# Attention scores and value products as small TensorE tiles of 64 rows

## The chip, the cores and the metric

The kernel runs on one core of one Trainium2 chip. The metric is the device time of the program in microseconds, the median of several runs. One more run was profiled: the trace of that one execution is what all rows below come from. Engines are called PE (TensorE, matmuls), PEld (its weight loads), DVE (VectorE), ACT (ScalarE), POOL (GpSimd) and SP (SyncE, which issues most transfers).

## What is computed

A local attention is followed by two feed-forward layers, all in float32. Batch is 4, there are 8 heads of 64 dimensions and 768 positions. Positions are cut into chunks of 32; the queries of a chunk see 16 positions to the left, the chunk itself, 8 to the right, and 8 memory positions, 64 keys in all.

```
for c in range(nc):                       # 24 chunks
    q_c   = q[:, :, 32*c : 32*c+32]
    k_full = concat(mem_k, k[:, :, max(0, 32*c-16) : min(S, 32*c+40)])
    v_full = the same of mem_v, v
    scores = q_c @ k_full.T / sqrt(64)
    a = exp(scores - max(scores)); a = a / (sum(a) + 1e-9)
    out[:, :, 32*c : 32*c+32] = a @ v_full

x = out as 3072 tokens x 512
h = x @ w_in;  g = max(0.01*h, h);  x = g @ w_out          # 512 -> 2048 -> 512
y = ((x @ w_a) * (x @ w_b)) @ w_out2                        # 512 -> 1536 -> 512
```

## The kernel before

Tokens are cut into 24 units of 128 (four chunks each, all eight heads) and into six blocks of 512 tokens (`bi`, four units each). The first feed-forward layer runs block after block: for each of 16 slices `f` of the hidden width, `mm1` computes h (L413 to L415, three matmuls of 128x128 weights over 512 columns, four times) and, two slices later, `mm2` adds it into four accumulators a (L533 to L537). The attention of block `bi + 1` is laid between the slices of block `bi` by the table `beside` (`at(bi, f, ...)`); the attention of units 0 to 3 comes first, in an order written out by hand (`InOrder`, whose instructions all have the line L47, or L44 for the first). From unit 4 on a scheduler sets the order on each engine. From 603 us on the last layers run, which the change does not touch.

For one unit the steps are these. `a_scores` multiplies queries and keys into the PSUM tile s (L277); `a_max`, `a_exp`, `a_soft1` and `a_soft2` make the softmax on DVE and ACT in the tile p; the probabilities are turned, keys onto the partitions, into PT, for units 0 to 7 by PE and a copy of ACT (`a_turn_mm`, L357, and `a_turn_copy`, L368), for later units by 16 DVE transposes of 32x32 pieces (`a_turn`, L346); `a_pv` multiplies them with the values into the PSUM tile pv (L386); `a_out` splits that into a high part on ACT (L399) and a low part on DVE (L400), the inputs xh and xl of the next block.

Two heads are handled in one matmul, with zeros: the queries of two heads stand in the two halves of the 128 rows, each in its own 32 of 64 weight columns, and the rest of the 64 columns is zero (`qs`, `qz`, set once on POOL and DVE). One matmul of scores thus has 128 rows, 64 weight columns (two heads of 32 queries) and 64 moving columns (keys); even and odd chunks write the lower and upper 64 PSUM partitions. In the value products the 64 weight columns are the dimensions of a head, the 64 moving columns two sets of 32 queries of PT, half of each zero. One unit has 16 matmuls of each kind. Each fp32 matmul shows as two records in the trace.

PSUM has eight banks of 512 floats for each partition: two for h (`ps_h`), two that scores, turned probabilities and products of units 2 and later take in turn (`ps_s`), four that hold a and, at the start, other things (`ps_a`).

Of the kernel before, what the change touches and what calls it, by code (L numbers as in the profile page):

```python
# [14 lines left out]
P = 128  # L15
# [38 lines left out]
def kernel(  # L54
# [28 lines left out]
        for n, b in (("ps_h", 2), ("ps_s", 2), ("ps_a", 4))  # L83
    ]
    ps_h, ps_s, ps_a = [p.__enter__() for p in psum1]
# [46 lines left out]
    class Weights:  # L132
# [70 lines left out]
    qz = ap_.tile([P, 16, 2 * CH], F32, tag="qz", name="qz", bufs=1)  # L203
    qs = [
        ap_.tile([P, 2 * CH, 16], F32, tag=t, name="qs", bufs=1) for t in ("pz", "ps", "pwa", "pwb")
# [3 lines left out]
    PT = [  # L209
        ap_.tile([P, 4, 4, 2, CH], F32, tag=f"pt{i}", name=f"pt{i}", bufs=1) for i in range(2)  # L210
    ]
    for t in qs[0:2]:
        nc.gpsimd.memset(t[0:64, CH:2 * CH, :], 0.0)
        dve.memset(t[64:128, 0:CH, :], 0.0)
    for t in PT:
        nc.gpsimd.memset(t[0:64, :, :, 1, :], 0.0)
        nc.gpsimd.memset(t[64:128, :, :, 0, :], 0.0)
    for t in qs[2:4]:
        nc.gpsimd.memset(t[0:64, CH:2 * CH, :], 0.0)
        nc.gpsimd.memset(t[64:128, 0:CH, :], 0.0)  # L220
    nc.gpsimd.memset(qz[0:64, :, CH:2 * CH], 0.0)
    nc.gpsimd.memset(qz[64:128, :, 0:CH], 0.0)
# [5 lines left out]
    def q_load(upto):  # L228
        while loaded[0] < min(upto, NU):
            u = loaded[0]  # L230
            if u < len(qs):
                eng = act if u < 1 else sp
                sp.dma_start(out=qs[u][0:64, 0:CH, :], in_=q_l[u, 0:64])
                eng.dma_start(out=qs[u][64:128, CH:2 * CH, :], in_=q_l[u, 64:128])
# [9 lines left out]
    def q_place(u, copy):  # L244
        if u >= NU:
            return
        t = qr.pop(u).rearrange("p q o -> p o q")
        qb = qz
        copy(qb[0:64, :, 0:CH], t[0:64])
        copy(qb[64:128, :, CH:2 * CH], t[64:128])  # L250
# [17 lines left out]
    def a_scores(u):  # L268
        qb = q_of(u)
        s = ps_s.tile([P, 8, 64], F32, tag="s", name="s")  # L270
        for cp in range(2):
            k = kt.pop((u, cp))
            for hp in range(4):
                for cpar in range(2):
                    o = (2 * cp + cpar) * 4 + hp
                    r = (cpar * 4 + hp) * 64
                    pe.matmul(  # L277
                        s[64 * cpar:64 * cpar + 64, cp * 4 + hp, :],
                        qb[:, o, :],
                        k[:, r:r + 64],  # L280
                        start=True, stop=True,
                    )
        st[u] = s
# [4 lines left out]
    def a_max(u):  # L288
        s = st[u]
        m = sm.tile([P, 8], F32, tag="m", name="m", bufs=2)  # L290
        dve.reduce_max(m, s, axis=AX.X)
# [3 lines left out]
        else:  # L295
            dve.tensor_tensor(
                out=p, in0=s, in1=m.unsqueeze(2).to_broadcast([P, 8, 64]), op=ALU.subtract
# [3 lines left out]
    def a_exp(u):  # L301
        s = st.pop(u)
        p, m = pt_[u]
        if u in by_scalar:
            l = sm.tile([P, 8], F32, tag="l", name="l", bufs=2)
            for r in range(8):
                act.activation(
                    p[:, r], s[:, r], AF.Exp, bias=m[:, r:r + 1], scale=scale,
# [11 lines left out]
    def a_soft2(u):  # L320
        p = pt_[u]
        if u % UPB == 0:
            dve.memset(p[0:64, 0:4, 0:LEFT], 0.0)
        if u % UPB == UPB - 1:
            dve.memset(p[64:128, 4:8, WIN - RIGHT:WIN], 0.0)
# [11 lines left out]
    def a_turn(u):  # L337
        p = pt_.pop(u)
        pt = PT[u % 2]
        for cpar in range(2):  # L340
            for hpar in range(2):
                i0 = 64 * cpar + 32 * hpar
                for hpx in range(2):
                    for b in range(2):
                        o0 = 64 * hpx + 32 * b
                        dve.transpose(  # L346
                            out=pt[o0:o0 + 32, :, 2 * cpar + hpar, hpx, :],
                            in_=p[i0:i0 + 32, hpx::2, 32 * b:32 * b + 32],
                        )
# [3 lines left out]
    def a_turn_mm(u, pool, tag):  # L353
        p = pt_.pop(u)
        ps = pool.tile([P, 4, 4, CH], F32, tag=tag, name="pT")
# [8 lines left out]
    def a_turn_copy(u, halves=(0, 1)):  # L364
# [5 lines left out]
    def a_turn_pe(u, pool, tag):  # L370
        a_turn_mm(u, pool, tag)
# [4 lines left out]
    def a_pv(u, pool, tag):  # L376
        pt = PT[u % 2]
        o = pool.tile([P, KC, UT], F32, tag=tag, name="pv")
        for cp in range(2):
            v = vt.pop((u, cp))  # L380
            for pair in range(2):
                for cpar in range(2):
                    for hpar in range(2):
                        i = ((cpar * 2 + hpar) * 2 + pair) * 64
                        t0 = (2 * cp + cpar) * CH
                        pe.matmul(  # L386
                            o[64 * hpar:64 * hpar + 64, 2 * pair:2 * pair + 2, t0:t0 + CH],
                            v[:, i:i + 64],
                            pt[:, 2 * cp + pair, 2 * cpar + hpar].rearrange("p h q -> p (h q)"),
# [6 lines left out]
    def a_out(u, blk, off):  # L396
        o = pvt.pop(u)
        hi, lo = x1[blk]
        act.copy(hi[:, :, off:off + UT], o)  # L399
        dve.tensor_tensor(  # L400
# [805 lines left out]
```

## Time and profile before

| | us |
|---|---|
| median of three runs | 1138.04 (1137.56 to 1139.1) |
| the profiled execution, whole | 1137.88 |
| its span in the trace | 1136.1 |
| PE busy | 1119.5 |
| DVE busy | 805.3 |
| ACT busy | 476.2 |

The page gives for each engine its busy time and share. Busy time of PE is from a record's start to its modelled end, and records overlap, so the cost of a group is read from the starts of what stands before and behind it in the timeline.

### The profile page before, as it was taken

Reading aid. Unit: us, or ns where it says so; the run is one execution under the profiler, and the core shown is the slowest. Engines: PE = TensorE matmul, PEld = TensorE weight load, DVE = VectorE, ACT = ScalarE, POOL = GpSimd, SP = SyncE. Lnnn points to the kernel's source line nnn. Section 1 sums busy time; section 2 is a strip of 40 time slices with the busy share of each in tenths; the row PEclk is TensorE's granted clock in tenths of the full one; section 3 lists DMA queues with packets and bytes.
Section 4 is the critical chain, followed back from the end, with each engine's and each line's share of the span. In section 5 each row is a group of like instructions: output and inputs, shape, how many; then the busy total and the mean of one; then the engine's idle time right before and its main releaser. Section 6 shows DMA issues by size and latency. Waiting matters only on the chain.

```text
span 1136.1 us, 18009 instructions
## 1 busy us (share of the span) xinstructions
PE 1119.5 (99%) x6992; PEld 956.9 (84%) x6992; DVE 805.3 (71%) x1485; ACT 476.2 (42%) x806; POOL 6.3 (1%) x16
## 2 busy tenths in 40 slices
PE   6899999999999999999999999999999999999998
PEld 6788888888888888888888898988898989898988
DVE  7999499889979964645112838598747689756777
ACT  5887555565554544325223424143333143333231
POOL 2000000000000000000000000000000000000000
PEclk9999999999999999999999999999999999999999
DMA  9988799999999985336236766667756567747451
GB/s 319 390 277 305 272 350 319 320 341 340 315 329 334 331 304 180 111 96 235 97 145 229 252 209 180 199 189 254 268 174 200 173 211 227 222 153 231 147 188 74
DMA packets 89380, 269.68 MB, mean 237 GB/s; under 512 B 9552, under 2 KB 10960, under 8 KB 88528
## 3 DMA queue, kind: packets, MB, share of 16 engines
q1 hardware_dynamic: 89216, 268.41, 70.1%
q8 instruction: 55, 0.90, 0.3%
q14 instruction: 29, 0.24, 0.1%
q10 hardware_dynamic: 80, 0.13, 0.0%
HBM read 214.50 MB, written 54.00 MB: 236 GB/s over the span
## 4 chain that ended last, share of the span: by engine, by line
PE 92%; DVE 3%; DMA 2%; ACT 2%; SPq 1%; issue 0%; DVEq 0%; ACTq 0%
PE h L413 8%; PE a L533 7%; PE a L536 7%; PE a L537 7%; PE h L414 7%; PE h L415 7%; PE A L874 4%; PE A L873 4%; PE A L875 4%; PE C L874 3%; PE C L873 3%; PE C L875 3%; PE oc L1012 2%; PE oc L1011 2%; PE oc L1010 2%; PE pv L386 2%
## 5 line engine op out<-in xcount | busy, mean ns | idle before, releaser
L413 PE MATMUL h<-xh,w 128*128 128x512 f32 (+1 forms) x384 | 151.5, 394 | 1.4 <-DVE w L183 0.7
L533 PE MATMUL a<-gh,w 128*128 128x512 f32 (+1 forms) x392 | 150.6, 384 | 0.5 <-DVE w L183 0.3
L536 PE MATMUL a<-gl,w 128*128 128x512 f32 (+1 forms) x392 | 150.4, 384 | 0.0
L537 PE MATMUL a<-gh,w 128*128 128x512 f32 (+1 forms) x392 | 150.4, 384 | 0.0
L414 PE MATMUL h<-xl,w 128*128 128x512 f32 (+1 forms) x384 | 148.5, 387 | 0.2 <-DVE xl L47 0.2
L415 PE MATMUL h<-xh,w 128*128 128x512 f32 (+1 forms) x384 | 148.5, 387 | 0.0
L511 DVE TENSOR_TENSOR gl<-g,gh 128x512 fp32r<-128x512 f32 (+1 forms) x96 | 65.2, 679 | 94.0 <-ACT gh L508 93.6
L899 ACT CAST st<-gb 128x512 fp32r<-128x512 f32 x114 | 69.4, 621 | 108.7 <-DVE gb L894 108.4
L505 ACT ACTIVATE g<-h 128x512 f32<-128x512 f32 (+1 forms) x96 | 56.3, 586 | 113.0 <-PE h L415 112.3
L890 ACT COPY u<-A 128x512 f32<-128x512 f32 x68 | 39.9, 586 | 115.8 <-PE A L875 115.8
L533 PEld LDWEIGHTS a<-gh,w 128*128 128x128 f32 x392 | 73.6, 188 | 15.6 <-ACT x L550 0.6
L413 PEld LDWEIGHTS h<-xh,w 128*128 128x128 f32 x384 | 72.1, 188 | 17.2 <-DVE w L183 0.9
L536 PEld LDWEIGHTS a<-gl,w 128*128 128x128 f32 x392 | 73.6, 188 | 14.5
L537 PEld LDWEIGHTS a<-gh,w 128*128 128x128 f32 x392 | 73.7, 188 | 14.5
L894 DVE TENSOR_TENSOR st<-gb,st 128x512 fp32r<-128x512 f32 x111 | 75.3, 690 | 13.5 <-ACT st L899 11.3
L415 PEld LDWEIGHTS h<-xh,w 128*128 128x128 f32 x384 | 72.1, 188 | 14.7
L414 PEld LDWEIGHTS h<-xl,w 128*128 128x128 f32 x384 | 72.2, 188 | 14.2 <-DVE xl L47 0.5
L346 DVE STREAM_TRANSPOSE pt<-p 32x128 f32<-32x128 f32 x256 | 77.4, 302 | 4.3
L873 PE MATMUL A<-ch,wab 128*128 128x512 f32 x204 | 79.5, 390 | 0.0
L874 PE MATMUL A<-cl,wab 128*128 128x512 f32 x204 | 79.5, 390 | 0.0
L875 PE MATMUL A<-ch,wab 128*128 128x512 f32 x204 | 79.4, 389 | 0.0
L508 ACT CAST gh<-g 128x512 fp32r<-128x512 f32 (+1 forms) x96 | 59.0, 615 | 2.7
(180 smaller groups left out, 2311.1 us busy)
## 6 DMA issues: line engine op xcount, KB each, us to landing
wab<-wab SPq DMA_DIRECT2D x126, 512.0 KB, 4.3
w<-wod SPq DMA_DIRECT2D x80, 512.0 KB, 4.8
raw<-w SPq DMA_DIRECT2D x68, 512.0 KB, 6.8
wt<-wtd SPq DMA_DIRECT2D x63, 512.0 KB, 4.7
k<-kl SPq DMA_DIRECT2D x48, 256.0 KB, 5.3
v<-vl SPq DMA_DIRECT2D x48, 256.0 KB, 5.7
wab<-pwb SPq DMA_DIRECT2D x12, 768.0 KB, 6.3
wod<-w SPq DMA_DIRECT2D x16, 512.0 KB, 5.6
```

What stands on the lines that cost most here:

```text
L346: dve.transpose(out=pt[o0:o0 + 32, :, 2 * cpar + hpar, hpx, :], in_=p[i0:i0 + 32, hpx::2, 32 * b:32 * b + 32],)
L413: pe.matmul(ps, w[1], x[0], start=first, stop=False)
L414: pe.matmul(ps, w[0], x[1], start=False, stop=False)
L415: pe.matmul(ps, w[0], x[0], start=False, stop=last)
L533: pe.matmul(ps, slot[:, 1, c], gh[:, t], start=f == 0 and o == 0, stop=False, **kw)
L536: pe.matmul(ps, slot[:, 0, c], gl[:, t], start=False, stop=False, **kw)
L537: pe.matmul(ps, slot[:, 0, c], gh[:, t], start=False, stop=f == NF1 - 1 or (o == HALF and f == LEAD - 1), **kw)
L873: pe.matmul(ps, w[:, 1, c], hi[:, kc], start=first and kc == 0, stop=False, **kw)
L874: pe.matmul(ps, w[:, 0, c], lo[:, kc], start=False, stop=False, **kw)
L875: pe.matmul(ps, w[:, 0, c], hi[:, kc], start=False, stop=kc == HC - 1, **kw)
L894: dve.tensor_tensor(out=out, in0=x, in1=y, op=op)
L899: act.copy(w[:, 0, :], t)
```

## The change

Scores and products are cut into matmuls of one head and one chunk. A score matmul takes 64 rows (one head's dimensions), 32 weight columns (32 queries) and 64 moving columns (keys); a product takes 64 rows (keys), 64 weight columns (dimensions) and 32 moving columns (queries). There are 32 of each per unit. The position in the array follows from the operands: the row half from the partitions they are read from (`hpar`, or `hpx`), the column part from the PSUM partitions they write. The two row halves write two different PSUM banks. The zeros are gone, and with them the memsets and one of two copies into `qz` and into PT; the queries of units 1 to 3 come in one transfer.

PSUM is handed out in pairs of banks (`pair`). Units 0 to 3 use one pair of `ps_s` and two of `ps_p`; then `open_acc` gives the four banks of `ps_p` to the accumulators. From unit 4 on there is one pair. `cluster` puts the products of a unit and the scores of the next into one pair, products in the first half of each bank, scores in the second; the turned probabilities of units 3 to 7 use the same pair between clusters.

```diff
-        for n, b in (("ps_h", 2), ("ps_s", 2), ("ps_a", 4))
+        for n, b in (("ps_h", 2), ("ps_s", 1), ("ps_p", 2))
...
-    qz = ap_.tile([P, 16, 2 * CH], F32, tag="qz", name="qz", bufs=1)
+    qz = ap_.tile([P, 16, CH], F32, tag="qz", name="qz", bufs=1)
...
-    for t in qs[0:2]:
-        nc.gpsimd.memset(t[0:64, CH:2 * CH, :], 0.0)
-        dve.memset(t[64:128, 0:CH, :], 0.0)
...
-        copy(qb[0:64, :, 0:CH], t[0:64])
-        copy(qb[64:128, :, CH:2 * CH], t[64:128])
+        copy(qz, qr.pop(u).rearrange("p q o -> p o q"))
...
+    def pair(pool):
+        return pool.tile([P, 2, 512], F32, tag="s", name="sv")
+
+    def a_scores(u, bank, half=0):
+        qb = q_of(u)
+        s = bank[:, :, 256 * half:256 * half + 256].rearrange("p b (r k) -> p b r k", k=64)
+        ks = [kt.pop((u, cp)) for cp in range(2)]
+        for cs in ((0, 1), (2, 3)) if u < 1 else (range(4),):
+            for hp in range(4):
+                for c in cs:
+                    for hpar in range(2):
+                        d = slice(64 * hpar, 64 * hpar + 64)
+                        r = ((c % 2) * 4 + hp) * 64
+                        pe.matmul(
+                            s[32 * c:32 * c + 32, hpar, hp, :],
+                            qb[d, 4 * c + hp, :],
+                            ks[c // 2][d, r:r + 64],
+                            start=True, stop=True,
+                        )
...
-        for h in halves:
-            d = slice(64 * h, 64 * h + 64)
-            act.copy(pt[d, :, :, h, :], ps[d])
+        act.copy(pt, ps)
...
+        o = bank[:, :, 0:256].rearrange("p x (a t) -> p x a t", a=2)
+        vs = [vt.pop((u, cp)) for cp in range(2)]
+        for a in range(2):
+            for c in range(4):
+                for hpar in range(2):
+                    for hpx in range(2):
+                        i = (((c % 2) * 2 + hpar) * 2 + a) * 64
+                        d = slice(64 * hpx, 64 * hpx + 64)
                         pe.matmul(
+                            o[64 * hpar:64 * hpar + 64, hpx, a, c * CH:c * CH + CH],
+                            vs[c // 2][d, i:i + 64],
+                            pt[d, 2 * hpar + a, c, :],
                             start=True, stop=True,
                         )
...
+    def cluster(u, n):
+        bank = pair(ps_s)
+        if u is not None:
+            a_pv(u, bank)
+        if n is not None:
+            a_scores(n, bank, 1)
```

How this moves instructions is shown at three places on PE.

The first is the middle of block 1, where the products of one unit and the scores of the next stand between the slices of the feed-forward layer. In the names, h and a are its results, xh and xl its inputs, gh and gl the parts of g, w a weight; before, s and pv are scores and products, and after, sv is the pair of banks for both. Before:

```order
L537 MATMUL a<-gh,w 128x512
L386 MATMUL pv<-pt_126,v 64x2x32 x16
L277 MATMUL s<-k,qz 64x64 x16
L413 MATMUL h<-xh,w 128x512
L414 MATMUL h<-xl,w 128x512
```

And now:

```order
L530 MATMUL a<-gh,w 128x512
L374 MATMUL sv<-pt_126,v 64x32 x32
L267 MATMUL sv<-k,qz 32x64 x32
L400 MATMUL h<-xh,w 128x512
L401 MATMUL h<-xl,w 128x512
```

The place is the same; the matmuls have doubled in number, and the two kinds now have different shapes. There are 15 such places, and five each where only scores or only products stand.

The second is unit 4, on PE behind the four transposes (pT before, the rows `sv<-id,p` now) that turn its probabilities. Before:

```order
L357 MATMUL pT<-id,p 128x128 x4
L413 MATMUL h<-xh,w 128x512
L414 MATMUL h<-xl,w 128x512
L415 MATMUL h<-xh,w 128x512
```

And now:

```order
L347 MATMUL sv<-id,p 128x128 x4
L374 MATMUL sv<-pt_126,v 64x32
L400 MATMUL h<-xh,w 128x512
L401 MATMUL h<-xl,w 128x512
L402 MATMUL h<-xh,w 128x512
...
L374 MATMUL sv<-pt_126,v 64x32 x31
L267 MATMUL sv<-k,qz 32x64 x32
```

One of the 32 products of unit 4 has come forward by 24 matmuls, to right behind the transposes; the other 31 stand where all 16 stood.

The third is unit 3 in the start, with the waits that the rows carry. Before:

```order
L47 MATMUL pT<-id,p 128x128 [waits DVE_49,PE_49,Activation_49]
L47 MATMUL pT<-id,p 128x128 x3
L47 MATMUL a<-gh,w 128x256 [waits DVE_49]
L47 MATMUL a<-gl,w 128x256 [waits Activation_49]
```

And now:

```order
L47 MATMUL sv<-id,p 128x128 [waits DVE_49]
L47 MATMUL sv<-id,p 128x128 [waits Activation_49] x3
L47 MATMUL a<-gh,w 128x256
L47 MATMUL a<-gl,w 128x256 [waits Activation_49]
```

The order is the same. The transposes write the pair of banks that the products of unit 2 used, so their wait for DVE now covers the reading of those products (`a_out(2)`), which stands behind `a_soft2(3)` in DVE's order; the wait of the first a is gone, since it is met earlier.

## Rows read from the trace of the kernel before

**Rows 1.** The page: span, and busy us (share of the span) xinstructions
```profile
span 1136.1 us, 18009 instructions
PE 1119.5 (99%) x6992; PEld 956.9 (84%) x6992; DVE 805.3 (71%) x1485; ACT 476.2 (42%) x806; POOL 6.3 (1%) x16
```

**Rows 2.** PE's waits from 36 us on: us in total, times, longest
```profile
PE h L413 <- DVE w L183: 0.7, 1, 0.7
...
PE a L533 <- DVE w L183: 0.3, 1, 0.3
...
PE a L533 <- ACT x L550: 0.2, 1, 0.2
```

**Rows 3.** Groups by shape, 60 to 530 us: busy us, mean ns | idle before
```profile
L386 PE MATMUL pv<-pt,v 128*64 128x64 f32 x640 | 23.0, 225 | 0.0
...
L277 PE MATMUL s<-k,qz 128*64 128x64 f32 x608 | 21.2, 223 | 0.0
```

**Rows 4.** Timeline of PE around 70 us: start us, us, line, weights, moving, records
```profile
69.47 0.39 PE L536 MATMUL a<-gl,w 128*128 128x512 f32 x1
69.70 0.39 PE L537 MATMUL a<-gh,w 128*128 128x512 f32 x1
70.02 1.15 PE L386 MATMUL pv<-pt,v 128*64 128x64 f32 x32
71.00 1.10 PE L277 MATMUL s<-k,qz 128*64 128x64 f32 x32
72.03 0.50 PE L413 MATMUL h<-xh,w 128*128 128x512 f32 x1
72.37 0.39 PE L414 MATMUL h<-xl,w 128*128 128x512 f32 x1
```

**Rows 5.** Timeline of PE from 70.01 to 70.03 us alone
```profile
70.02 0.28 PE L386 MATMUL pv<-pt,v 128*64 128x64 f32 x2
```

**Rows 6.** Timeline of PE in the start: fillers of 128 columns
```profile
11.79 1.50 PE L47 MATMUL warm<-id 128*128 128x128 f32 x12
```

**Rows 7.** Weight loads by shape, 15 to 36 us: busy us, mean ns
```profile
L47 PEld LDWEIGHTS h<-xh,w 128*128 128x128 f32 x24 | 3.9, 189 | 1.0 <-ACT xh L47 0.9
...
L47 PEld LDWEIGHTS pv<-pt,v 128*64 128x64 f32 x96 | 3.1, 138 | 0.4 <-ACT pt L47 0.3
```

**Rows 8.** Timeline of PE at the transposes of unit 4
```profile
63.96 0.63 PE L357 MATMUL pT<-id,p 128*128 128x128 f32 x4
64.34 0.48 PE L413 MATMUL h<-xh,w 128*128 128x512 f32 x1
```

**Rows 9.** Timeline of ACT there
```profile
64.97 1.18 ACT L368 COPY pt<-pT 64x512 f32<-64x512 f32 x2
```

**Rows 10.** Timeline of PE at unit 3, in the start
```profile
30.78 0.63 PE L47 MATMUL pT<-id,p 128*128 128x128 f32 x4 [0.98 <-ACT g L47]
31.89 0.39 PE L47 MATMUL a<-gh,w 128*128 128x256 f32 x1 [0.49 <-DVE w L47]
...
33.52 1.15 PE L47 MATMUL pv<-pt,v 128*64 128x64 f32 x32
```

**Rows 11.** Timeline of DVE in the start
```profile
28.61 0.69 DVE L47 SCALAR_TENSOR_TENSOR z<-raw,z 128x512 int32<-128x512 int32 x1
29.50 0.17 DVE L47 TENSOR_SCALAR l<-l 128x8 f32<-128x8 f32 x1 [0.19 <-ACT p L47]
...
31.75 0.68 DVE L47 TENSOR_TENSOR xl<-pv,xh 128x512 fp32r<-128x512 f32 x1
```

**Rows 12.** Chain of work in the start, in order of time: start us, us
```profile
12.32 8.18 DMA raw<-w
...
26.99 2.48 ACT p L47 x16
```

**Rows 13.** Stretch 60 to 85 us: PE, PEld, DVE, ACT, POOL busy, PEclk, DMA, GB/s
```profile
60.00:85.00 25.00, 25.00 (x169) 20.48 (x168) 24.86 (x50) 20.03 (x34) 0.00 (x0) 1.00 0.89 292
```

**Rows 14.** Timeline of PE behind the scores of unit 4
```profile
44.95 0.39 PE L533 MATMUL a<-gh,w 128*128 128x256 f32 x1 [0.30 <-DVE w L183]
```

More of the change, by code (lines that the diff above doesn't have):

```diff
@@ L202 @@
     ident = sm.tile([P, P], F32, tag="id", name="id", bufs=1)
[L203 removed]
+    qz = ap_.tile([P, 16, CH], F32, tag="qz", name="qz", bufs=1)
     qs = [
[L205 removed]
+        ap_.tile([P, CH, 16], F32, tag=t, name="qs", bufs=1) for t in ("pz", "ps", "pwa", "pwb")
     ]
[L209 to L222 removed]
+    PT = [ap_.tile([P, 4, 4, CH], F32, tag=f"pt{i}", name=f"pt{i}", bufs=1) for i in range(2)]
     kt, vt, st, qr = {}, {}, {}, {}
@@ L231, in q_load @@
             if u < len(qs):
-                eng = act if u < 1 else sp
-                sp.dma_start(out=qs[u][0:64, 0:CH, :], in_=q_l[u, 0:64])
-                eng.dma_start(out=qs[u][64:128, CH:2 * CH, :], in_=q_l[u, 64:128])
+                if u < 1:
+                    sp.dma_start(out=qs[u][0:64], in_=q_l[u, 0:64])
+                    act.dma_start(out=qs[u][64:128], in_=q_l[u, 64:128])
+                else:
+                    sp.dma_start(out=qs[u], in_=q_l[u])
             else:
@@ L296, in a_max @@
             dve.tensor_tensor(
-                out=p, in0=s, in1=m.unsqueeze(2).to_broadcast([P, 8, 64]), op=ALU.subtract
+                out=p.rearrange("p (b r) k -> p b r k", b=2), in0=s,
+                in1=m2.unsqueeze(3).to_broadcast([P, 2, 4, 64]), op=ALU.subtract,
             )
@@ L339, in a_turn, with a_turn_mm @@
         pt = PT[u % 2]
[L340 to L349, printed above, removed]
+        for c in range(4):
+            for hpx in range(2):
+                for b in range(2):
+                    o0 = 64 * hpx + 32 * b
+                    dve.transpose(
+                        out=pt[o0:o0 + 32, :, c, :],
+                        in_=p[32 * c:32 * c + 32, hpx::2, 32 * b:32 * b + 32],
+                    )
     turned = {}
-    def a_turn_mm(u, pool, tag):
+    def a_turn_mm(u, pool):
         p = pt_.pop(u)
-        ps = pool.tile([P, 4, 4, CH], F32, tag=tag, name="pT")
+        ps = pair(pool)[:, 0].rearrange("p (r c q) -> p r c q", r=4, c=4)
         for r in range(4):
@@ L397, in a_out @@
         o = pvt.pop(u)
-        hi, lo = x1[blk]
-        act.copy(hi[:, :, off:off + UT], o)
-        dve.tensor_tensor(
-            out=lo[:, :, off:off + UT], in0=o, in1=hi[:, :, off:off + UT].bitcast(F32),
-            op=ALU.subtract,
-        )
+        hi, lo = [
+            x[:, :, off:off + UT].rearrange("p (a x) t -> p x a t", x=2) for x in x1[blk]
+        ]
+        act.copy(hi, o)
+        dve.tensor_tensor(out=lo, in0=o, in1=hi.bitcast(F32), op=ALU.subtract)
     def x_tiles(key):
@@ L442 @@
     q_load(3)
-    warm = ps_a.tile([P, TB], F32, tag="a", name="warm")
+    warm = ps_h.tile([P, TB], F32, tag="h", name="warm")
     def fill(n):
@@ L448, in fill @@
             pe.matmul(warm[:, 0:P], ident, ident, start=True, stop=True)
-    a_scores(0)
-    a_scores(1)
+    a_scores(0, pair(ps_s))
+    a_scores(1, pair(ps_p))
     fill(6)
@@ L462 @@
     a_soft2(0)
-    a_turn_mm(0, ps_a, "a")
+    a_turn_mm(0, ps_p)
     fill(6)
     a_max(1)
-    a_turn_copy(0, (0,))
+    a_turn_copy(0)
     a_exp(1)
-    a_turn_copy(0, (1,))
     W1.bias(2)
-    a_pv(0, ps_h, "h")
+    a_pv(0, pair(ps_s))
     v_load(6)
@@ L476 @@
     a_out(0, ("x", 0), 0)
-    a_turn_mm(1, ps_a, "a")
-    a_scores(2)
+    a_turn_mm(1, ps_p)
+    a_scores(2, pair(ps_p))
     a_turn_copy(1)
@@ L483 @@
     a_max(2)
-    a_pv(1, ps_h, "h")
+    a_pv(1, pair(ps_s))
     v_load(8)
@@ L493, with open_acc @@
     acc = {}
+    def open_acc():
+        psum1.pop().__exit__(None, None, None)
+        psum1.append(
+            tc.tile_pool(name="ps_a", bufs=4, space=bass.MemoryType.PSUM, reuse_waits="tile")
+        )
+        acc["pool"] = psum1[-1].__enter__()
     def mm1_pe(bi, parts):
@@ L522, in mm2 @@
         if bi not in acc:
-            acc[bi] = [ps_a.tile([P, TB], F32, tag="a", name="a") for _ in range(KC)]
+            acc[bi] = [acc["pool"].tile([P, TB], F32, tag="a", name="a") for _ in range(KC)]
         gh, gl = g
@@ L589, in first_items @@
         W1.bias(5)
-        a_scores(3)
+        a_scores(3, pair(ps_p))
         a_max(3)
         W1.low(3)
-        a_turn_mm(2, ps_a, "a")
+        a_turn_mm(2, ps_p)
         a_turn_copy(2)
@@ L596, in first_items @@
         h1 = mm1_pe(0, parts[1])
-        a_pv(2, ps_s, "s")
+        a_pv(2, pair(ps_s))
         W1.join()
@@ L616, in first_items @@
         W1.low(5)
-        a_pv(3, ps_s, "s")
+        a_pv(3, pair(ps_s))
         W1.join(0)
```

64 lines of the change are left out of this document (23 added, 41 removed).

## The prediction

> **What bounds the kernel now.** I read the page first: TensorE (PE) is busy for 1119.5 us of a span of 1136.1 us [rows 1]. Then the list of what PE waited for from 36 us on: five lines, 1.9 us in all, and none of them names a tile of the attention [rows 2]. So from 36 us to the end the time is the sum of what PE issues, and a change is worth what it takes out of that sum. The third view groups PE's instructions by shape: between 60 and 530 us the value products (pv, 20 units) and the scores (s) of the same units are 640 and 608 records [rows 3]; one matmul of fp32 leaves two records, so a unit has 32 of each kind. "Unit" below is 128 tokens; there are 24, of which units 0 to 3 run in the first 36 us and units 4 to 23 between 43 and 507 us.
>
> What one unit costs is read from the timeline around 70 us [rows 4]. The 32 records of s span 1.10 us, of which the last is 0.22 us long by itself: 0.88 us for 31 starts, 28 ns each; pv gives 0.93/31 = 30 ns. I use 29 ns, so 32 records are 0.93 us, and pv and s together cost PE about 1.9 us per unit: 37 us for 20 units, 3.3% of the span. That is all the change can touch after the start.
>
> **How the array is used now.** A filler matmul, 128 columns wide and alone in the array, leaves 12 records in 1.50 us, the last 0.28 long: 111 ns each [rows 6]. Half of that, for 64 columns, would be 56 ns, yet records of pv follow each other every 29 ns. And in a window of 20 ns at 70.02 two of them start [rows 5]. So the two column halves already work side by side: one record holds its half for 2 x 29 = 58 ns. The weight load in front of each record lies beneath it: a load of 128 columns lasts 189 ns, one of 64 columns 138 ns [rows 7], so 64 more columns take 51 ns (0.8 ns a column), which just fits under 58.
>
> **The change, part by part.**
>
> *Scores.* 32 matmuls of 64 rows by 32 columns instead of 16 of 128 by 64: 64 records per unit, each still moving 64 columns, with a weight load of 32 columns (26 ns). A record should hold its tile for the same 58 ns, but eight tiles are named in turn. If all eight run side by side, 64 x 58 / 8 = 464 ns instead of 928: 0.46 us less per unit. Nothing in the trace shows more than two tiles at once, so the bounds come from the nearest rows: 64 records at 29 ns each, 1.86 us (0.93 more), on the one side, 0.46 us on the other. I take 0.46: two starts inside 20 ns [rows 5] say that the issue is much faster than one per 29 ns, and what spaces the pairs is the 58 ns of a tile. Unit 4 I leave out: right behind it PE already waits 0.30 us for VectorE's weights [rows 14], so an earlier end there becomes a longer wait. 19 x 0.46 = **-8.7 us**.
>
> *Value products.* 32 matmuls of 64 by 64: 64 records, four tiles, each moving 32 columns, half as many (28 ns by the filler's 111 ns for 128). But each still loads 64 weight columns, and that is 51 ns per record by rows 7. So a tile is held by its loads, not by its stream: 64 x 58 / 4 = 928 ns, **0**. With the bare 51 ns it would be 816 ns, a gain of 0.11 per unit, 2.2 us in all; that end I keep for the range.
>
> *A switch of tile shape.* Today s follows pv in one shape, without a gap (0.98 us from the first pv to the first s, against 0.93 for the records alone). Going between the full array and the half costs: 0.32 us instead of 0.23 from the last full matmul to the first pv, 1.03 instead of 0.93 from the first s to the first full matmul, and 0.34 instead of 0.23 behind that [rows 4]; 0.09 on the way in, 0.21 on the way out. The change puts one more switch, 64x64 to 64x32, into the 15 places where pv and s stand together (first order piece). I take 0.15 each, **+2.2 us**, between 0 (no drain between two tilings) and 3.2. The Trainium skill, "TensorEngine Tiling (Array Packing)", section Key Properties, says that changing the tiling mode, not just the tile, drains TensorE. The 0.09 to 0.21 us in rows 4 agree for the switch from and to the full array; for two tilings with each other no row here shows it.
>
> *One pv matmul that stands early.* In unit 4 the order puts one pv matmul right behind the four transposes (second piece). It needs ScalarE's copy of their result. In the trace that copy begins at 64.97 and takes two pieces of 0.59 [rows 9]; the change makes it one, so it ends near 65.56. Today PE goes on with h at 64.34 [rows 8]. So PE stands 1.2 us, and pays two more switches, 0.3: **+1.6 us** (0.9 to 2.5).
>
> *The start.* The halves of units 0 to 3 are worth nothing by themselves: the chain there runs over a weight load from 12.32 to 20.5 us and ScalarE's exponentials up to 29.47 [rows 12]. Merging two copies into one takes 0.58 off ScalarE ahead of the second of these, of which VectorE, busy until 29.3, can use 0.2 [rows 11]. Against that, the scores, the transposes and the products now share one pair of banks: unit 3's transposes wait until VectorE has read the products of unit 2 (third piece: the first transpose waits for VectorE). That subtraction runs from 31.75 to 32.43 [rows 11], the transposes began at 30.78 and a followed at 31.89 [rows 10]. Now they begin near 32.25, and a at 32.25 + 4 x 0.11 = 32.7: **+0.8 us** (-0.5 to +1.5, the low end if fewer query transfers let the weights land sooner).
>
> *At nothing.* The memsets that go were on GpSimd and on VectorE, while VectorE waited for the first scores. ScalarE's two query copies per unit become one; no line in PE's waits names them. VectorE is the engine to watch: 24.86 of 25 us between 60 and 85 [rows 13]. If PE ran ahead there it would wait for weights; but up to 110 us PE gains 3 x 0.46 and loses 3 x 0.15 and 1.6, so it does not run ahead.
>
> Sum: -8.7 + 2.2 + 1.6 + 0.8 = -4.1 us. The profiled execution took 1137.88 us; 1133.8 with the change. The median of the three runs, 1138.04, is 0.16 above it: **1133.9 us**.
>
> **Rivals.**
>
> *The products halve too.* If the loads of the four tiles do not set the pace, 64 x 30 / 4 = 480 ns: 0.45 us less in 20 units, 9.0 us, 1124.9 us. For it: fewer columns move. Against it: the 51 ns of rows 7. Chance 0.14.
>
> *The scores gain nothing.* If LDWEIGHTS and MATMUL can be issued no faster than the 29 ns per two records in a pair that the trace sustains, or only four tiles overlap, s stays at 0.93 and only the price remains: 2.2 + 1.6 + 0.8 = +4.6, 1142.6 us. This is also the case in which the change doesn't do what it says. Chance 0.13.
>
> *Slower: the two row halves of a column take turns.* Nothing in the trace shows two row tiles at once; the two that overlap differ in columns. If row tiles share the path of weights or data, s has four tiles' worth (0.93, no gain), but pv only two: 64 x 58 / 2 = 1.86 us, 0.93 more in 20 units, 18.6 us. With the price, +23.2: 1161.2 us. It decides from the point where a pv record follows the one before by more than 14.5 ns. Chance 0.12.
>
> *Slower: every record costs 29 ns, whatever its tile.* Then s and pv both double: 39 x 0.93 + 4.6 = +41, 1179 us. Rows 5 speak against it. Chance 0.06. The Trainium skill, "TensorE: Matmul & The Clock Gate", section "Wait — 56ns, not 53.3ns?", states that starts are never closer than about 25 ns however few columns move; by that s and pv would cost 64 x 25 ns = 1.6 us each, an estimate from that page, and the kernel would come to about 1169 us; the chance of 0.06 stands for this too. The trace disagrees for starts on different tiles: two in 20 ns [rows 5].
>
> **How the numbers follow.** My forecast, scores halved and products unchanged, has 0.52; its own range is 1129.5 to 1137.5 from the bounds above. Products halved too 0.14, nothing gained 0.13, row tiles in turn 0.12, 29 ns each 0.06, anything else 0.03. The range leaves out the two slow cases: **1123 to 1144**, which keeps 0.79. A measurement of this kernel tells 0.2% (2.3 us) from no change, so faster is below 1135.8: 0.46 of the forecast's 0.52 and the 0.14, 0.60. Slower, above 1140.3, is the three other cases, 0.31. Within 0.2%: 0.09.
>
> **What would show it.** In the profile after, the scores of a unit should be 64 records in about 0.7 us from first start to last end, 7 ns apart, and pv 64 records in about 1.15, 15 ns apart; if pv takes about 0.7, its loads were not the bound. From the first pv to the first s should be some 1.1 us. PE's waits should have a new line of about 1.2 us for ScalarE's copy near 64 us and a longer one for VectorE near 31 us. The granted clock, 1.00 (the level of 2.4 GHz) in the stretch of rows 13, should stay there. The prediction is wrong if pv takes over 1.5 us (row tiles in turn), or if s is no shorter than 1.1 us.

## The result, and the profile after

The changed kernel takes 1144.52 us (median of 8 runs, 1141.69 to 1148.38); the kernel before, run beside it, 1138.18 (1137.56 to 1139.36). The ratio is 1.0056, 95% interval 1.0045 to 1.0068. It is slower by 6.3 us; the forecast was 1133.9, with 1144 as the upper end.

The profiled execution of it took 1141.8 us, 2.7 less than the median. First the page, which answers to [rows 1]: span, then busy us, share of the span and instructions.

```profile
span 1139.8 us, 21024 instructions
PE 1117.0 (98%) x8528; PEld 952.6 (84%) x8528; DVE 803.7 (71%) x1483; ACT 447.8 (39%) x778; POOL 0.2 (0%) x4
```

PE is busy for 2.5 us less, in a span that is 3.7 us longer: PE now stands more than it saves. Next the stretch of block 1 that answers to [rows 4], in PE's timeline (start, us, line, weights, moving, records), and under it a place where scores stand alone.

```profile
93.27 0.39 PE L530 MATMUL a<-gh,w 128*128 128x512 f32 x1
93.59 1.14 PE L374 MATMUL sv<-pt,v 64*64 64x32 f32 x64
94.65 0.86 PE L267 MATMUL sv<-k,qz 64*32 64x64 f32 x64
95.44 0.50 PE L400 MATMUL h<-xh,w 128*128 128x512 f32 x1
...
243.27 0.39 PE L530 MATMUL a<-gh,w 128*128 128x512 f32 x1
243.59 0.86 PE L267 MATMUL sv<-k,qz 64*32 64x64 f32 x64
244.38 0.50 PE L400 MATMUL h<-xh,w 128*128 128x512 f32 x1
```

The kernel before at the second place:

```profile
239.12 0.39 PE L537 MATMUL a<-gh,w 128*128 128x512 f32 x1
239.44 1.15 PE L277 MATMUL s<-k,qz 128*64 128x64 f32 x32
240.52 0.50 PE L413 MATMUL h<-xh,w 128*128 128x512 f32 x1
```

What the attention costs PE at a place is the time from the start of the last full matmul before it to the start of the first one behind it, less the 0.23 us that one full matmul takes. Products and scores together: 95.44 - 93.27 - 0.23 = 1.94 us, against 72.03 - 69.70 - 0.23 = 2.10 [rows 4]. Scores alone: 244.38 - 243.27 - 0.23 = 0.88, against 1.17. Added up in this way over all places from 42 to 520 us, with the waits that lie inside them (0.8 and 0.7 us, 0.3 in the kernel before), it is 42.7 us where it was 45.4: **2.7 us gained**. So the tiles do what they were made for, if less than forecast, and the loss stands elsewhere. PE's waits from 36 us on answer to [rows 2]:

```profile
PE h L401 <- DVE xl L390: 2.1, 2, 1.3
PE a L526 <- DVE w L183: 0.8, 1, 0.8
...
PE sv L374 <- ACT pt L356: 0.7, 1, 0.7
PE h L400 <- DVE w L47: 0.5, 1, 0.5
```

The wait for ScalarE's copy pt in unit 4 is the forecast one. The 2.1 us for xl are new: they stand where a block of 512 tokens ends. But the largest piece comes ahead of this list. The start, in PE's timeline, answers to [rows 10]:

```profile
18.07 1.12 PE L47 MATMUL sv<-pt,v 64*64 64x32 f32 x60
22.50 0.43 PE L47 MATMUL sv<-pt,v 64*64 64x32 f32 x4 [3.31 <-issue]
23.60 0.58 PE L47 MATMUL h<-xh,w 128*128 128x256 f32 x1 [0.68 <-ACT xh L47]
...
35.52 0.66 PE L47 MATMUL sv<-id,p 128*128 128x128 f32 x4 [2.67 <-DVE xl L47]
...
39.38 0.49 PE L400 MATMUL h<-xh,w 128*128 128x512 f32 x1 [0.70 <-ACT xh L47]
```

Two new stands. At 19.2 us PE stops in the middle of unit 1's products, 60 records done and four to go, for 3.31 us, and the profile knows nothing that it waited for ("issue"). At unit 3's transposes it waits 2.67 us for VectorE. The kernel before at the same two h:

```profile
19.75 0.38 PE L47 MATMUL h<-xh,w 128*128 128x256 f32 x1 [0.78 <-ACT xh L47]
...
35.36 0.50 PE L413 MATMUL h<-xh,w 128*128 128x512 f32 x1 [0.68 <-ACT xh L47]
```

The first h of 512 columns starts 4.0 us later (39.38 against 35.36), and of that 3.85 us are there at the first h of 256 columns (23.60 against 19.75): in this execution it is mostly the first stand that puts the start back. The table of stretches has one thing more (from:to, length, then PE, PEld, DVE, ACT and POOL busy, the granted clock, DMA share, GB/s):

```profile
20.81:27.63 6.82, 4.31 (x64) 3.65 (x65) 4.03 (x9) 4.04 (x20) 0.00 (x0) 0.50 1.04 411
```

PE stood from 19.2 to 22.5, and from 20.8 to 27.6 the granted clock was 0.50, the level of 1.2 GHz. In the kernel before it stayed at 1.00.

The bill of the profiled execution: start +4.0, attention on PE -2.7, waits behind the start that lie in no place of the attention +1.7 (2.1 + 0.5, less the 0.7 + 0.2 of [rows 2]); sum +3.0, and the span grew by 3.7. The other 0.7 us is not placed. The median lies 2.7 us higher than this execution, and no trace shows where; the mean granted clock of the eight runs goes from 0.999 (1141.7 us) down to 0.994 (1148.4 us), and stood at 0.997 in the profiled one.

### The profile page after: what moved, and what is told of

It reads as the page before. It is cut to its first block, busy times and chain, and to the rows that moved or that the text cites. A ratio compares the mean times of both kernels' runs of the same rounds, so it can differ in the third digit from the quotient of the medians.

```text
span 1139.8 us, 21024 instructions
## 1 busy us (share of the span) xinstructions
PE 1117.0 (98%) x8528; PEld 952.6 (84%) x8528; DVE 803.7 (71%) x1483; ACT 447.8 (39%) x778; POOL 0.2 (0%) x4
## 4 chain that ended last, share of the span: by engine, by line
PE 68%; DVE 5%; ACT 1%; issue 0%; DVEq 0%; ACTq 0%
PE A L879 4%; PE A L880 4%; PE A L878 4%; PE h L400 4%; PE a L529 4%; PE a L530 4%; PE a L526 4%; PE h L401 4%; PE h L402 4%; PE C L879 3%; PE C L880 3%; PE C L878 3%; PE oc L1017 2%; PE oc L1016 2%; PE oc L1015 2%; PE oc L47 2%
## 5 line engine op out<-in xcount | busy, mean ns | idle before, releaser
L498 ACT ACTIVATE g<-h 128x512 f32<-128x512 f32 (+1 forms) x96 | 56.5, 588 | 115.9 <-PE h L402 115.8
```

## Experiments

Each is the changed kernel with one thing undone or moved, unless it says otherwise. "Old start" means that units 0 to 3 keep the matmuls, zeros, banks and order of the kernel before, and that the pair of banks is opened behind them. The kernel before ran beside each, at 1137.7 to 1138.1 us.

**Where is it lost: start or later?** The old start.

```diff
-    a_scores(0, pair(ps_s))
-    a_scores(1, pair(ps_p))
+    a_scores(0)
+    a_scores(1)
...
+        open_later()
         return [(0, parts[1], g1), (0, parts[2], g2)]
```

> The changed kernel with units 0 to 3 exactly as in the kernel before (128-row matmuls with zeros, the old tiles in PSUM, the old order); units 4 to 23 as changed. Theory (the loss sits in the start): in the changed kernel's trace the first 512-column matmul of h starts at 39.38 us, 4.0 later than the 35.36 of before; inside this lie 3.3 us in which PE stands in the middle of unit 1's products, during which a 16 KB packet of the instruction queue arrives (20.25 to 21.13 us), and the 6.8 us that follow at a granted clock of 0.50 (1.2 GHz). With the old start that matmul should start at 35.4 again, the granted clock of the run be 1.00, and the median fall by 4 to 7 us against the changed kernel's 1144.5, to 1137 to 1140, with a spread of runs as narrow as before's (about 2 us, not 7). Rival (the loss is in the attention units after the start): h at 35.4, but the median stays above 1142.

Measured: 1145.27 us (ratio 1.0063, 1.0049 to 1.0077). The first h did come early, at 36.76, and the time did not fall: as a story of the start alone, my first theory was wrong. (In the profiled runs of all kernels with the old start the first h comes between 35.2 and 36.9 us, so a single trace tells the start to about 1 us.) The granted clock, too, was not back at 1.00: it fell for 3.4 us from 26.08 us, behind waits of PE of 0.74 and 0.99 us, and twice where blocks end. PE's waits, and these two stretches:

```profile
PE h L525 <- DVE xl L498: 2.5, 1, 2.5
PE sv L486 <- DVE pt L459: 2.0, 4, 0.9
```

```profile
220.65:224.04 3.39, 3.39 (x10) 2.64 (x9) 3.32 (x7) 0.04 (x1) 0.00 (x0) 0.50 0.92 312
...
326.50:329.80 3.30, 3.30 (x10) 2.52 (x9) 1.97 (x4) 0.67 (x1) 0.00 (x0) 0.50 1.02 384
```

How the wait of 2.5 comes about is seen in the timelines of PE, ACT and DVE there:

```profile
316.17 1.14 PE L486 MATMUL sv<-pt,v 64*64 64x32 f32 x64
325.83 0.50 PE L525 MATMUL h<-xl,w 128*128 128x512 f32 x1 [2.48 <-DVE xl L498]
...
321.69 0.62 ACT L126 CAST pwa<-pz 128x512 fp32r<-128x512 f32 x1 [5.35 <-DMA wtd<-pwa]
322.22 0.58 ACT L497 CAST xh<-sv 128x512 fp32r<-128x512 f32 x1
...
324.49 0.68 DVE L127 TENSOR_TENSOR pwa<-pz,pwa 128x512 fp32r<-128x512 f32 x1
325.09 0.68 DVE L498 TENSOR_TENSOR xl<-sv,xh 128x512 fp32r<-128x512 f32 x1
```

The block's last products are done at 317.3. ScalarE's xh stands behind a cast of the weight preparation that waits 5.35 us for a transfer; VectorE's xl stands behind the preparation too and starts at 325.09, and PE, at the next block's h, waits for it. In the kernel before the same two do not stand behind such a wait:

```profile
315.26 0.58 ACT L399 CAST xh<-pv 128x512 fp32r<-128x512 f32 x1
...
317.29 0.68 DVE L400 TENSOR_TENSOR xl<-pv,xh 128x512 fp32r<-128x512 f32 x1
```

The code names them in the same place; the scheduler's order differs.

**Is it the block ends?** Each unit of blocks 1 to 4 one slice earlier, with the old start and with the changed start.

```diff
-        for k, f in enumerate([5, 8, 11, 14] if bi == 0 else [2, 5, 8, 11]):
+        for k, f in enumerate([5, 8, 11, 14] if bi == 0 else [1, 4, 7, 10]):
```

> The kernel with the old start (1145.3 us) with the same shift of each unit by one slice. Theory of the block ends: its waits of 2.5 us for xl and 2.0 us for the turned probabilities and the two stretches of 3.4 us at a granted clock of 0.50 go, 7 us in all, so 1136.5 to 1139; against the changed kernel with the same shift it then shows what the start alone costs, 2 to 4 us. Rival (block ends matter little): above 1143.

> The changed kernel with one number per unit different: in blocks 1 to 4 each unit's attention stands one slice of the feed-forward layer earlier (slices 1, 4, 7, 10 instead of 2, 5, 8, 11), so that a block's last products come at slice 13, one slice (about 6 us) further ahead of the next block's first h. Theory (what the old start did not give back is lost where a block ends: VectorE and ScalarE hold weight preparation ahead of the split of the last unit's products, PE waits for xl and the granted clock falls behind that, as the traces with the old start show at 220 and 326 us): no wait for xl L390 in PE's list, no 0.50 stretch after 36 us, and the median falls by 3 to 5 us, to 1139.5 to 1141.5, what is left being the start. Rival (the start makes all of the loss, by chance equal in the kernels with the old start): within 1 us of 1144.5.

With the old start 1139.21 us (1.0013, 1.0005 to 1.0022): 6.1 us back, a little less than expected, and no line for xl L498 in PE's waits. So there the block ends made most of the loss. With the changed start 1144.69 us (1.0062, 1.0048 to 1.0075), as slow as unshifted: that expectation failed. Its trace has no wait for xl at block ends, but one of 1.1 us for the transposes, and its start came out worse (a stand of 3.6 us, first h at 40.49, and a second stretch at 0.50 from 36.22 to 39.63 us behind a wait of 1.9 us for xl). With the same shift, then, the changed start costs 1144.69 - 1139.21 = **5.5 us**. What the block ends cost in the changed kernel itself I can put no higher than the 2.1 us of its waits.

**What in the start: banks or instructions?** The changed banks, but the old matmuls in units 0 to 3; unshifted and shifted. The diff is against the old start.

```diff
-        s = ps_s.tile([P, 8, 64], F32, tag="s", name="s")
+        s = bank[:, 0].rearrange("p (r k) -> p r k", k=64)
```

> The same, but in units 0 to 3 only the matmuls and their zeros are the old ones: the banks are those of the changed kernel (scores, turned probabilities and products in pairs of banks, one pair of them shared by the products of unit 2 and the transposes of unit 3). Theory A (the number of PE instructions makes the loss, since PE runs dry of them): no stand of 3.3 us, granted clock 1.00, and only the wait for VectorE's xl ahead of unit 3's transposes stays: first h of 512 columns at 36.0 to 37.0, the median 0.5 to 1.5 us above the kernel with the old start. Theory B (the shared banks make the loss): first h at 38 to 39.5, the median within 1.5 us of the changed kernel.

> The changed kernel with its banks in the start and its tiles from unit 4 on, the shift of one slice, and in units 0 to 3 alone the old matmuls of 128 rows. With the shift, the old start and its old banks gave 1139.2 us and the changed start 1144.7; this one divides the 5.5 us. Theory A (PE's instructions, of which units 0 to 3 now have the old number, make most of it; the shared banks make the 0.8 us of the prediction): 1139.5 to 1141, no stand of PE in the start on 'issue' above 1 us, first h of 512 columns at 37 to 38 us. Theory B (the shared banks make most of it): 1143 to 1145, first h at 39 us or later.

Unshifted 1147.13 us (1.0076, 1.0063 to 1.0089): no stand on "issue" above 0.51 us, but the first h came at 37.59, between the two theories, and the granted clock fell to 0.50 from 32.4 us, which theory A excluded. Its block ends (5.2 us for xl in three waits) hide the rest, and its median is outside of both theories; by itself it decides nothing. Shifted 1142.13 us (1.0042, 1.0029 to 1.0056), between the two theories. It divides the 5.5 us: 1142.13 - 1139.21 = 2.9 for the banks, 1144.69 - 1142.13 = 2.6 for the rest of the changed start, which is the tiles with their doubled instructions, and with them the copies, zeros and query transfers that went. Each is good to about 2 us (the intervals 1.0029 to 1.0056 and 1.0048 to 1.0075 overlap), so which of them is larger stays open; and in the changed kernel's own trace the first stand makes nearly all of the start, so the two need not simply add. In its trace of the start:

```profile
33.41 0.66 PE L47 MATMUL sv<-id,p 128*128 128x128 f32 x4 [2.70 <-DVE xl L47]
36.06 1.98 PE L47 MATMUL sv<-pt,v 128*64 128x64 f32 x32
38.72 0.50 PE L514 MATMUL h<-xh,w 128*128 128x512 f32 x1 [0.69 <-ACT xh L47]
```

```profile
34.59:37.98 3.39, 3.39 (x40) 3.03 (x38) 1.72 (x3) 2.45 (x5) 0.00 (x0) 0.50 0.98 300
```

The shared pair of banks makes one wait of 2.70 us, where the kernel before had two of 0.98 and 0.49 at the same place [rows 10], and the granted clock falls to 0.50 behind it: unit 3's products take 1.98 us for 1.15. First h at 38.72, against 36.69 with the old banks; the last 0.9 of the 2.9 us stands later.

**Does PE run out of instructions?** The kernel before, with more PE instructions in the start and nothing else.

```diff
-    fill(6)
+    for n in range(64):
+        c = 32 * (n % 4)
+        pe.matmul(
+            warm[c:c + 32, 0:32], ident[0:64, 0:32], ident[0:64, 0:32], start=True, stop=True
+        )
     a_max(1)
```

> The kernel before, with the second group of six fillers of 128 columns (24 PE instructions) replaced by 64 matmuls of 64 rows, 32 weight columns and 32 moving columns on four tiles in turn (256 instructions, about 1.9 us by 14.5 ns a record). It has then about as many PE instructions in the first 20 us as the changed kernel. Theory (PE runs dry of instructions in the start because they are fetched behind transfers that fill the DMA engines): a stand of PE of 1 to 4 us with no releaser but 'issue' between 14 and 24 us, during which a packet of the instruction queue lands, first h of 512 columns at 37 to 39 us instead of 35.4, median 1.5 to 4 us above before. Rival (the number of instructions costs nothing): first h at 35.4 to 36.5, median within 1 us of before.

Measured: 1141.68 us (1.0034, 1.002 to 1.0047), 3.9 us above before, first h at 38.98. PE's timeline, and the DMA queues within the second stand, 15.25 to 18.25 us (packets, MB, share of 16 engines' time):

```profile
12.71 1.29 PE L47 MATMUL warm<-id 64*32 64x32 f32 x128
14.63 0.59 PE L47 MATMUL pv<-pt,v 128*64 128x64 f32 x13 [0.64 <-issue]
18.30 1.33 PE L47 MATMUL pv<-pt,v 128*64 128x64 f32 x19 [3.08 <-issue]
```

```profile
q1 hardware_dynamic: 498, 1.13, 103.6%
q8 instruction: 1, 0.02, 2.1%
```

The 64 small matmuls themselves took less time than the fillers (1.29 us, not 1.50). The loss is the stand of 3.08 us, again in the middle of a unit's products with nothing that the profile shows to wait for, again with one packet of the instruction queue inside it (0.02 MB), and with the data queue filling the DMA engines. The window 18.13 to 21.53 us then has a granted clock of 0.50. The changed kernel's stand has the same sign, from 19.25 to 22.45 us:

```profile
q1 hardware_dynamic: 486, 1.29, 102.2%
q8 instruction: 1, 0.02, 1.7%
```

So a start with more instructions is enough to make such a stand in the old kernel, and with the old number of them in the changed banks it is gone. Two counts say that it is the instruction stream that PE waits for. Over a whole run one packet goes with some 255 records of PE, matmuls and weight loads together (55 packets for 13984 records before, 67 for 17056 after). And the stands keep a count, not a time: 697 such records lie ahead of the stand in the changed kernel, 697 again in the shifted one, and 442 here, 255 fewer. In the changed kernel the packet moves from 20.25 to 21.13 us and PE goes on at 22.50; in all three kernels PE goes on 1.4 to 1.6 us behind the packet's end. Why the packet comes late is not shown. That it stands behind the data transfers is argued from the full DMA engines, but these are as full in the kernel before (a share of 1.02 to 1.05 from 15 to 36 us), which has no such stand, and no run took the transfers away.

**What are the two kinds of tiles worth?** Old start; scores alone, or products alone, in tiles.

```diff
-                    for hpx in range(2):
...
-                            o[64 * hpar:64 * hpar + 64, hpx, a, c * CH:c * CH + CH],
-                            vs[c // 2][d, i:i + 64],
-                            pt[d, 2 * hpar + a, c, :],
+                        o[64 * hpar:64 * hpar + 64, a, :, c * CH:c * CH + CH],
+                        vs[c // 2][:, i:i + 64],
+                        pt[:, 2 * hpar + a, c].rearrange("p h q -> p (h q)"),
```

> Old start; from unit 4 on the scores in tiles of 64 by 32, the products in the old matmuls of 128 rows (with zeros), both in the pair of banks. Theory (the products gain nothing from their tiles, 0.92 us against 0.93, and any switch of shape costs about 0.1 us): the scores take 0.64 us from first to last start (0.88 before), the products 0.93, and the median is within 1 us of the kernel with the old start and both in tiles. Rival (the product tiles gain, hidden so far by the switch): 1 to 3 us slower than that kernel.

> Old start; from unit 4 on the products in tiles of 64 by 64, the scores in the old matmuls of 128 rows (with zeros), both in the pair of banks. Theory: the products take 0.92 us for 64 records, the scores 0.88 as before, and 15 switches of about 0.1 us come on top, so nothing is gained: 3 to 6 us slower than the kernel with scores alone in tiles (20 times 0.24 us missing). Rival (the score tiles bring nothing outside the trace): within 1 us of it.

Scores alone: 1137.35 us (0.9997, 0.9988 to 1.0005). Products alone: 1141.65 us (1.0033, 1.002 to 1.0045), 4.3 us slower, as expected. The first expectation failed: it is 7.9 us faster than the kernel with both (1145.27). PE's cost per place does not explain that (1.96 us here, 1.94 with both); the traces differ in the order, with no wait for xl and no stretch at 0.50 here. That the order makes all of the 7.9 us is argued, not shown. Per place, PE's timeline of the two:

```profile
160.47 0.39 PE L646 MATMUL a<-gh,w 128*128 128x512 f32 x1
160.79 1.15 PE L484 MATMUL sv<-pt,v 128*64 128x64 f32 x32
161.87 0.86 PE L412 MATMUL sv<-k,qz 64*32 64x64 f32 x64
162.66 0.50 PE L522 MATMUL h<-xh,w 128*128 128x512 f32 x1
```

```profile
161.17 0.39 PE L653 MATMUL a<-gh,w 128*128 128x512 f32 x1
161.49 1.14 PE L491 MATMUL sv<-pt,v 64*64 64x32 f32 x64
162.56 1.15 PE L417 MATMUL sv<-k,qz 128*64 128x64 f32 x32
163.64 0.50 PE L529 MATMUL h<-xh,w 128*128 128x512 f32 x1
```

1.96 us with scores in tiles, 2.24 with products in tiles, 2.10 with neither. Scores gain 0.29 where they stand alone, so the switch takes 0.15 of it here; products in tiles gain 0.02 and pay 0.15 for the switch.

**How long is a tile held?** The matmuls of a unit in other orders: `todo` lists them by row half, by pairs of columns, or tile by tile.

```diff
+        if way == 1:
+            todo = [(hp, c, hpar) for hpar in range(2) for hp in range(4) for c in range(4)]
...
+        elif way == 3:
+            todo = [(hp, c, hpar) for c in range(4) for hpar in range(2) for hp in range(4)]
```

> The kernel with the old start, where the matmuls of a unit come in other orders: units 4 to 11 as changed (eight tiles in turn for scores, four for products), 12 to 15 one row half after the other (four and two tiles in turn), 16 to 19 scores in pairs of column tiles (four in turn, both row halves) and products one column half after the other (two in turn, both row halves), 20 to 23 one tile at a time. Nothing is left out. My forecast's model (a tile is held 58 ns by a record, nothing else): scores 7 ns a record with eight tiles, 14.5 with four, 58 with one; the trace of the changed kernel has already shown 10.2 with eight. Theory 1 (the tile is still the limit, held 81 ns): 20 ns with four, 81 with one. Theory 2 (PE issues a record at most every 10 ns, the tile is held 58): 14.5 with four, 58 with one. Products: held 58 ns, so 14.5 with four, 29 with two, 58 with one; if row halves of a column share something, two row halves in turn are slower than two column halves.

One run, 1166.3 us. PE's timeline; scores alone with four tiles in turn (of one row half; pairs of columns give the same 0.99) and with one; then products with two column halves in turn (two row halves give the same 1.85) and with one tile. Units 4 to 11 are as changed: 0.86 for scores with eight tiles, 1.14 for products with four.

```profile
243.00 0.99 PE L424 MATMUL sv<-k,qz 64*32 64x64 f32 x64
...
441.64 2.40 PE L424 MATMUL sv<-k,qz 64*32 64x64 f32 x64
...
260.46 1.85 PE L508 MATMUL sv<-pt,v 64*64 64x32 f32 x64
...
482.68 3.30 PE L508 MATMUL sv<-pt,v 64*64 64x32 f32 x64
```

The last record is 0.22 us long. Products: 0.92 us, 1.63 and 3.08 from first to last start, or 15, 26 and 49 ns a record with four, two and one tile; the tile is the limit, and two row halves cost what two columns do. Scores: 12 ns with four tiles, 35 with one, but 10 with eight where half of 12 would be 6. So from four tiles to eight only 0.13 us come of the 0.38 that a tile limit would give: something else sets the pace there.

These are means, and a tile's turn runs into the next one's. Single records say it better: where one tile is used by itself, its starts, but for the first gap of 80, are 55 to 59 ns apart, scores and products alike, and four tiles in turn give four starts in 56 to 58 ns. So the forecast's 58 ns for a tile hold, and theory 1 (81 ns) falls. With eight tiles the changed kernel's scores at 243.59 us begin as forecast: the first 32 records start within 0.24 us, most of them 7 ns apart. Then come gaps of 26 and 56 ns, and the other 31 start within 0.32 us, 11 ns apart on the mean. Other units show the same pattern. So it is not a least distance of 10 ns either, as theory 2 had it. What holds up the second half, no run shows.

One thing more stands in this trace: the granted clock fell to 0.50 for 3.4 us from 485.85, 509.74 and 533.63 us, at or just behind the end of three of the four units' products in one tile at a time, and PE had not waited at all ahead of it.

**Other cures, and the regrouping alone.** The split of a unit's products written ahead of the next unit's softmax (old start, both in tiles); and the pair of banks and the clusters with old matmuls everywhere.

```diff
+            if k:
+                at(bi, f, load_v, u - 1)
+                at(bi, f, n_out, u - 1, ("x", bi + 1), (k - 1) * UT)
             at(bi, f, load_qk, u)
             at(bi, f, n_soft1, u)
```

> The kernel with the old start and both kinds in tiles (1145.3 us), with one change of order: beside a slice, the split of a unit's products into xh and xl is written ahead of the loads and the softmax of the next unit, not behind them; no shift of slices. Theory of the block ends (any order in which the split of a block's last unit stands less late on VectorE and ScalarE gives the 6 us back that the shift gave): 1137.5 to 1140, PE's wait for xl under 0.5 us. Rival (the block ends are late for the products' own length, not for the order): 1143 to 1146.

> Old start; from unit 4 on old matmuls of 128 rows for scores and products, but in the pair of banks and with products and scores in one cluster, as the change places them: no tile of 64 rows anywhere. It tells what the regrouping costs without the tiles. Theory: per unit PE pays what it pays in the kernel before (2.11 us for products and scores together), and what is left is the order at block ends: 1138 to 1141. Rival (the regrouping is free): within 0.5 us of before.

1141.51 us (1.0032, 1.002 to 1.0044): 3.8 back, less than expected; PE still waits 1.8 us for xl (in the profiled run, at 1144.03 us the slowest of its six). So order matters, and this is the lesser cure. The regrouping alone: 1139.43 us (1.0015, 1.0006 to 1.0024), 1.7 slower than before, with 2.10 us per place, as in the kernel before; it is not free.

**What is left when only the good part stays.** Old start, scores alone in tiles, one slice earlier.

> Old start, scores alone in tiles, products in the old matmuls of 128 rows, and every unit of blocks 1 to 4 one slice earlier: what the runs so far say is the best of the parts. The scores cost PE 0.29 us less per unit where they stand alone and 0.14 less beside products (counted from the trace of the kernel with scores alone in tiles), 20 units, 3.5 us; the start has the old number of PE instructions. If the two waits of 0.4 to 0.75 us at the block ends of that kernel (1137.35 us) go too: 1135 to 1137, faster than before by 1 to 3 us. Rival (the shift makes new waits elsewhere): 1137 to 1139.

1135.69 us against 1137.69, ratio **0.9978** (0.9969 to 0.9986): faster than both kernels. PE's waits from 36 us on are then four lines, 2.2 us in all, none for a tile of the attention, as in [rows 2].

## Why the prediction was wrong, step by step

- *What bounds the kernel.* Right for the kernel before [rows 1, 2]. But I carried "nobody waits at the attention" over to another order. The sum of what PE issues did fall; the time did not follow.
- *Scores.* Right in kind, too large: 0.29 us per unit where I took 0.46, some 5.5 us for 19 units and not 8.7. A tile was held 55 to 59 ns by a record, as forecast, and the first half of a unit's scores came at the forecast's 7 ns; the pause behind it and the slower second half make the mean 10.
- *Products.* Right: 0.92 us for 64 records, 15 ns each, a gain of 0.02. That it is the weight load, not the stream, that holds the tile was the reason given; no run tells the two apart.
- *The switch.* Right: 0.15 us at each of the 15 places, in all three pairs of shapes that the runs have.
- *The early product of unit 4.* Right in mechanism, 1.0 us for 1.6 (worked out as above from the two places where the products of unit 4 stand). The wait for the copy was 0.68 us of it:

```profile
68.77 0.30 PE L374 MATMUL sv<-pt,v 64*64 64x32 f32 x2 [0.68 <-ACT pt L356]
```

- *The start.* This step failed: +0.8 forecast, 5.5 measured with the block ends out of the way. The shared banks were named and mis-sized: a wait of 2.7 us and a stretch at half clock, 2.9 us in all, good to about 2. I had placed VectorE's xl by the kernel before and taken the waits there as given, and had not asked what the clock does when PE stands that long. The other 2.6 us, as uncertain, were not on my list: the rest of the changed start, of which PE's doubled instructions are the part that a run shows to stop PE (3.9 us in the kernel before). "The halves of units 0 to 3 are worth nothing by themselves" was true of the stream and left out its length in instructions.
- *At nothing.* Wrong too. VectorE was watched for PE running ahead; what came was a changed order on VectorE and ScalarE where a block ends, 2.1 us in the changed kernel's trace and 6 us with the old start. Nor had the sum a term for the regrouping into one pair of banks, which alone took 1.7 us.
- *The rivals.* None of them is what happened. "The scores gain nothing" had nearly the time (1142.6) and not the cause: the scores did gain, so that nearness is luck. The Trainium skill, "TensorE: Matmul & The Clock Gate", section "Wait — 56ns, not 53.3ns?", would have put starts at 25 ns or more; the traces show 10 and 15 ns on different tiles, so that rival falls as [rows 5] said.
- *What would show it.* Several signs named were there (pv as forecast, 1.06 us from the first pv to the first s, the wait for the copy though 0.7 us and not 1.2, the longer wait for VectorE). The scores took 0.86 us and not 0.7. And the granted clock held in the stretch of [rows 13], where I looked, and fell in the start, where I did not.

## What to carry to other kernels

A change that doubles an engine's instructions can have a cost that no duration shows: count the instructions of the start, where transfers fill the DMA engines, and look for a stand on "issue" with an instruction packet inside it. A wait of PE costs more than its length when the granted clock falls behind it, so price the two together. And where a scheduler sets the order, look again at the work that an untouched consumer waits for; here the last split of each block moved behind work that nobody needed yet, and placing it a slice earlier gave 6 us back with the old start, and nothing with the changed one.

## What the hardware showed that I had not expected

- PE stopped for 3.1 to 3.6 us on nothing that the profile shows, in three kernels with many instructions in the first 20 us; each time one packet of the instruction queue lay inside, and the stands came after 697, 697 and 442 matmul and weight-load records, one packet's 255 apart. The data queues took 102 to 104% of the DMA engines, but as much in the kernel before. The kernels with the old number had no such stand above 0.65 us in the start.
- During or behind stands of PE of 2.7 to 3.6 us in the start the granted clock went to 0.50 (1.2 GHz) for 3.4 to 6.8 us; at a block end two waits of 0.9 and 0.4 us within unit 11's products were followed by 3.4 us at 0.50. But waits alone do not tell it: it held behind the changed kernel's own wait of 2.67 us at 35.5 us and, in the kernel with the tile orders, behind the same two waits of 0.9 and 0.4 us, and there it fell three times where PE had not waited, behind products on one tile at a time.
- With one tile in use records started 55 to 59 ns apart, with four or eight in turn down to 7. On the mean of a unit eight tiles of 64 by 32 in turn gave 10 ns a record, four 12, one 35; four tiles of 64 by 64 15, two 26, one 49. A switch between two shapes cost 0.15 us, between the 0.09 and 0.21 of one from and to the full array [rows 4].
